# Attention scores of one token tile: two half-tile stages of four heads, or one stage of eight heads in alternation

## The chip, the cores and the metric

The kernel runs on one core of one Trainium2 chip. Five engines work side by side and meet at semaphores: TensorE (PE in the profile, its weight loads PEld), VectorE (DVE), ScalarE (ACT), GpSimd (POOL) and SyncE (SP), which here only issues DMAs. The metric is the device time of the kernel in microseconds (us); 2203.22 us is the median of three runs of the kernel before (2202.75 to 2208.09).

## The reference

Three layers follow each other, in float32, on 2304 tokens (4 batches of 576) with 512 features:

```python
k_p = k.reshape(B, H, 72, 8, D).mean(axis=3)          # keys and values pooled by 8
v_p = v.reshape(B, H, 72, 8, D).mean(axis=3)
scores = scale * np.matmul(q, k_p.transpose(0, 1, 3, 2))   # 8 heads of 64, 576 x 72
attn = softmax(scores)
x = np.matmul(attn, v_p)                               # -> 2304 x 512
x = (sigmoid(x @ w_gate) * (x @ w_val)) @ w_out        # first mixture layer, d_ff 1536
out = sum over e of P[:, e] * (relu(x @ w1[e]) @ w2[e])    # second: 8 experts, P by 8 Sinkhorn rounds
```

The change touches only the line that computes `scores`.

## The kernel before, in words

The tokens are cut into six blocks of 384 (`TB`), a block into three tiles of 128. In the first mixture layer the work is a list of 72 steps, `steps1`, one for a block j and a piece f of 128 of the 1536 inner features. A step issues, on PE, twelve matmuls for the gate ("g", L791), twelve for the value ("v"), and then the twelve of the output product of the step before it (`x2_step`, L533 to L565, shown as L543). The DVE and the ACT turn g and v into the hidden piece (L800 to L807). The second layer fills the rest of the time from about 680 us on, and is not touched.

All of it is under a schedule written out by hand: each engine executes its instructions in the order in which the program issues them. Three things are fitted into the steps.

The weights of the first layer come in as 36 wide pieces of 64-bit numbers. `narrow_tick` (L150 to L186) turns one into float32 on ACT, DVE and sometimes POOL, `split_chunk` (L213) then makes a high and a low part (L231 on ACT, `wa_lo`, L236, on DVE or POOL). The ACT queue also issues the DMA that saves the narrow form (L233), and the buffer `made` has four places, which become free only when that DMA has landed. The estimates `until["pe"]` and `until["dve"]` decide how many ticks are issued ahead of their need.

The attention of blocks 1 to 5 is the generator `attention`, cut into stages by `yield`. `slot(k, upto)` is called three times in a step: after g (k = 0), after v (k = 1) and at the step's end (k = 2). Each call adds a share, `left / (3 * (steps left) - k - 3)`, to `credit`, with `left` counted down from `STAGES`, and runs one stage for each whole credit, four at most. After the last scores of a block `hold` keeps the generator still for one or three steps. A block that is not ready when its first step begins is finished on the spot (L774).

For each tile and for g = 0 (even heads, partitions 0 to 63 of q and k) and g = 1 (odd heads, partitions 64 to 127), `scores` (L339) takes one PSUM bank, issues four head products of 64 rows, two instructions each in the trace (eight; a tile that crosses a batch has sixteen of half the width), and puts `less_max` (L367) on the list `post`: a maximum (L369) and a subtraction (L370) on DVE, which free the bank. `flush` empties the list when the next stage runs. Block 0 runs before the steps, and there `less_max` has its exponentials on ACT (L374). While the steps run, `at_bank` hands out the two banks "at" in turn; `turn_a` (transposes, L418), `values` (L433) and `after_block` (logits of a finished block, L598 to L618, through `side_bank`) use the same two. `softmax` (L389) is put on `later` after the last scores, and is issued between L804 and L807 of the next v, or at the first `turn_a` if that comes before.

Of the kernel before, what the change touches and what calls it, by code (L numbers as in the profile page):

```python
# [9 lines left out]
F32 = mybir.dt.float32  # L10
# [10 lines left out]
def attention_moe_moe_kernel(  # L21
# [31 lines left out]
    nc = tc.nc  # L53
# [7 lines left out]
    SP = S // POOL  # L61
# [23 lines left out]
    def bank(tag, bufs):  # L85
        return ps.tile([128, 512], F32, tag=tag, name=tag, bufs=bufs)
# [11 lines left out]
    def f32(ap):  # L98
        return ap.bitcast(F32)
# [38 lines left out]
    until = {"dve": 0, "pe": 0}  # L138
# [141 lines left out]
    def at_bank():  # L280

        n_bank[0] += 1
        if steps_on:
            return bank("at", 2)
        return bank(*AT_BANKS[n_bank[0] % len(AT_BANKS)])

    AT_BANKS = [("at", 2), ("big", 4), ("gv", 2), ("big", 4)]
    steps_on = []
    now = [0]
    hold = [0]  # L290

    def attention(at):
        kp, vp, qs, krs, vrs = {}, {}, {}, {}, {}
        e_ts, dens, a_ts = {}, {}, {}
# [38 lines left out]
        def pieces(j, t):  # L333

            c = j * TB + t * 128
            n = min(128, S - c % S)
            return [(0, n, c // S)] + ([(n, 128, c // S + 1)] if n < 128 else [])

        def scores(j, t, g):  # L339


            if (t, g) == (0, 0):
                e_ts[j] = at.tile([128, TPB, H, SP], F32, tag="e", name="e", bufs=1)
                dens[j] = at.tile([128, TPB, H], F32, tag="den", name="den", bufs=2)
            e_t = e_ts[j][:, t, 4 * g : 4 * g + 4]
            pt = at_bank()
            sc = pt[:, 0 : 4 * SP].rearrange("p (h s) -> p h s", h=4)
            for c0, c1, b in pieces(j, t):
                for i in range(4):
                    pr = slice(64 * g, 64 * g + 64)  # L350
                    nc.tensor.matmul(  # L351
                        out=sc[c0:c1, i],
                        lhsT=qs[j, t][pr, i, c0:c1],
                        rhs=kp[b][pr, i],
                        start=True,
                        stop=True,
                    )
            if g:
                del qs[j, t]
            elif (j, t) != (0, 0):  # L360
                load_q(j + (t + 3) // TPB, (t + 3) % TPB)
            m = at.tile([128, 4], F32, tag="mx", name="mx", bufs=4)
            until["pe"] += 900
            until["dve"] += 950
            post.append(lambda: less_max(j, t, g, sc, m, e_t))

        def less_max(j, t, g, sc, m, e_t):  # L367
            if j:
                nc.vector.tensor_reduce(out=m, in_=sc, axis=AX.X, op=ALU.max)  # L369
                nc.vector.tensor_sub(out=e_t, in0=sc, in1=m.unsqueeze(2).to_broadcast([128, 4, SP]))  # L370
                return
            nc.vector.tensor_reduce(out=m, in_=sc, axis=AX.X, op=ALU.max, negate=True)
            for i in range(4):
                nc.scalar.activation(  # L374
                    out=e_t[:, i],
                    in_=sc[:, i],
                    func=AF.Exp,
                    bias=m[:, i : i + 1],
                    accum_out=dens[j][:, t, 4 * g + i : 4 * g + i + 1],
                )  # L380


        post = []

        def flush():
            while post:
                post.pop(0)()

        def softmax(j, t):  # L389

# [75 lines left out]
        for hp in range(HP):  # L466
            load_k(1, hp)
        for t in range(TPB):
            for g in range(2):
                scores(0, t, g)  # L470
                flush()
        narrow_tick()
        narrow_tick()
        for t in range(TPB):
# [16 lines left out]
        for j in range(1, NBLK):  # L491
            b = (j * TB + TB - 1) // S
            if (j * TB - 1) // S < b:
                for hp in range(0, HP, 2):
                    pool_k(b, hp)
                    pool_k(b, hp + 1)
                    yield None
                for i in range(4):
                    pool_v(b, i)
                    if i % 2:  # L500
                        yield None
            for t in range(TPB):
                for g in range(2):
                    scores(j, t, g)
                    yield None
                    flush()
            later.append(lambda j=j: softmax(j, slice(0, TPB)))
            hold[0] = now[0] + 1 + 2 * (j > 1)
            yield None
            nb = ((j + 1) * TB + TB - 1) // S  # L510
            if j + 1 < NBLK and nb > b:
                for hp in range(HP):
                    load_k(nb, hp)
                for i in range(4):
                    load_v(nb, i)
            for t in range(TPB):
                for g in range(2):
                    turn_a(j, t, g)
                    yield None
                    flush()  # L520
                yield j
                values(j, t)
                if t < TPB - 1:
                    yield None
                flush()
            yield -1
# [183 lines left out]
    with tc.manual_schedule():  # L710
# [4 lines left out]
        at = at_pool.__enter__()  # L715
# [5 lines left out]
        def stage(upto=NBLK):  # L721

            if mark[0] is None or mark[0] < upto:
                mark[0] = next(stages, NBLK)
                n_ready[0] += mark[0] == -1
# [4 lines left out]
        def slot(k, upto):  # L730
# [9 lines left out]
            if j < NBLK:  # L740
                left = max(1, STAGES - n_stage[0])
                credit[0] = min(credit[0] + left / max(1, 3 * (at_step[j, 0] - n) - k - 3), 4)
# [2 lines left out]
                    stage(upto)  # L745
                    n_stage[0] = n_stage[0] + 1 if n_ready[0] == j else 0

        STAGES = 20

        while n_ready[0] == 0:  # L750
            stage()
# [9 lines left out]
        for n, (j, f) in enumerate(steps1):  # L761
            now[0] = n
            if (j, f) == (NBLK - 1, 0):
                assert next(stages, "end") == "end"
                at_pool.__exit__(None, None, None)
                pools["late"] = ctx.enter_context(tc.tile_pool(name="late", bufs=1, reuse_waits="tile"))
                load_w1(0)
                load_w1(1)
                first_w = prep_w1(0)
            if j == NBLK - 1 and 2 <= f < 9:  # L770
                load_xf(0, (0, 3, 4, 2, 6, 1, 5)[f - 2])
            if j == NBLK - 1 and f >= NF1 - 4:
                next(first_w, None)
            if n_ready[0] <= j:  # L774
                while n_ready[0] <= j:
                    stage()
                n_stage[0] = 0
                until["pe"] = max(until["pe"], until["dve"])
            upto = 3 if n <= at_step[0, NF1 - 1] else max(4, j + 2)
            pg = bank("gv", 2)  # L780
            pv = bank("gv", 2)
            g = base.tile([128, TB], F32, tag="g", name="g", bufs=2)
            hi, lo = h_tiles()
            for key, pt in (("g", pg), ("v", pv)):
                while (key, j, f) not in wsplit:
                    if not split_chunk() and not load_chunk():
                        narrow_tick()
                    until["pe"] = max(until["pe"], until["dve"])
                w = wsplit[key, j, f]
                mm(  # L790
                    pt[:, :TB],  # L791
                    [
                        (tuple(t[:, kk * 128 : (kk + 1) * 128] for t in w[:2]), tuple(t[:, kk] for t in xs1[j]))
                        for kk in range(KT)
                    ],
                )
                drop((key, j, f))
                until["pe"] += 2080
                if key == "g":
                    nc.scalar.activation(out=g, in_=pg[:, :TB], func=AF.Sigmoid)  # L800
                else:
                    until["dve"] = max(until["dve"], until["pe"]) + 1100
                    nc.vector.tensor_tensor(out=g, in0=g, in1=pv[:, :TB], op=ALU.mult)  # L803
                    nc.scalar.activation(out=hi, in_=g, func=AF.Copy)  # L804
                    while later:
                        later.pop(0)()
                    nc.vector.tensor_sub(out=lo, in0=g, in1=f32(hi))  # L807
                slot(key == "v", upto)
            if prev is not None:
                until["pe"] += 2080  # L810
                x2_step(*prev)
                if prev[1] == NF1 - 1:
                    gate = chain(gate, after_block(prev[0], prev[0] in (1, 3, 5)))
            gs[j, f] = (hi, lo)
            prev = (j, f)
            next(gate, None)
            slot(2, upto)
            stream(3)
# [135 lines left out]
        for n, (p, e, q) in enumerate(steps2):  # L954
# [36 lines left out]
            c1 = c_tile()  # L991
# [107 lines left out]
```

## Time and profile before

| what | value |
|---|---|
| median of three runs | 2203.22 us |
| the profiled execution | 2207.01 us, span 2205.2 us |
| PE busy | 2104.4 us (95%) |
| DVE busy | 1420.0 us (64%) |
| ACT, POOL busy | 881.9 us, 891.0 us (40% each) |
| mean granted clock of TensorE | 0.973 |

Busy shares are means over the whole span; the first layer, up to some 690 us, and the second have different limits. In a timeline row stand the start, the duration, the engine, the line of the kernel, the operation, the output and inputs by the program's names, their shape and how many instructions were merged; in brackets how long the engine sat idle before it and what it waited for.

### The profile page before, as it was taken

How to read it: one execution, taken by the hardware profiler on the slowest of the kernel's cores; microseconds unless marked ns; L12 is line 12 of the kernel's file. 1: busy time of each engine (PE TensorE's matmuls, PEld its weight loads, DVE VectorE, ACT ScalarE, POOL GpSimd, SP SyncE). 2: the span in 40 equal slices, each digit the busy share in tenths (PEclk: the TensorE clock that was granted, in tenths of full speed). 3: DMA queues.
4: the chain of work that ended last, by engine and by line, in shares of the span. 5: the costliest groups of instructions: out<-in, count | busy, mean ns of one | idle time of the engine just before them, and what ended most of it. 6: DMA issues, size and time to landing. Idle time of an engine off the chain costs nothing.

```text
span 2205.2 us, 28654 instructions
## 1 busy us (share of the span) xinstructions
PE 2104.4 (95%) x10973; PEld 1910.4 (87%) x10973; DVE 1420.0 (64%) x2162; ACT 881.9 (40%) x1607; POOL 891.0 (40%) x780
## 2 busy tenths in 40 slices
PE   4588889999999999999999999999999999999999
PEld 4478889988998898988888889888888888888888
DVE  6735787643534877666666666666666666666665
ACT  4233334344444444343434343434343434333332
POOL 1100000244454465545454545454544444454541
PEclk8679899999999999999999999999999999999999
DMA  7423453343482132212125212121224212121211
GB/s 227 150 63 110 144 167 129 125 162 130 134 290 92 58 111 81 77 58 77 58 77 186 77 58 77 59 76 59 76 65 175 93 66 74 61 77 58 77 58 39
DMA packets 87450, 222.09 MB, mean 101 GB/s; under 512 B 8848, under 2 KB 8848, under 8 KB 87312
## 3 DMA queue, kind: packets, MB, share of 16 engines
q1 hardware_dynamic: 82128, 210.81, 29.0%
q10 hardware_dynamic: 5184, 9.44, 1.1%
q8 instruction: 86, 1.41, 0.3%
q14 instruction: 52, 0.43, 0.1%
HBM read 189.55 MB, written 30.67 MB: 100 GB/s over the span
## 4 chain that ended last, share of the span: by engine, by line
PE 88%; DVE 6%; issue 2%; ACT 2%; DMA 1%; POOL 0%; SPq 0%; ACTq 0%; DVEq 0%; POOLq 0%
PE big L915 36%; PE at L884 18%; PE gv L884 14%; PE gv L268 12%; PE big L543 6%; PE at L351 1%; DVE wa_lo L236 1%; PE at L433 1%; DMA narrow<-made 1%; DVE made L166 1%; DVE wide L175 0%; PE at L268 0%; DVE g L803 0%; PE at L418 0%; ACT h L804 0%
## 5 line engine op out<-in xcount | busy, mean ns | idle before, releaser
L915 PE MATMUL big<-w2hl,h 128*128 128x512 f32 x3456 | 893.0, 394 | 0.0
L915 PEld LDWEIGHTS big<-w2hl,h 128*128 128x128 f32 x3456 | 641.2, 188 | 102.4
L944 DVE SCALAR_TENSOR_TENSOR acc<-big,prob,acc 128x512 f32<-128x512 f32 x516 | 385.5, 747 | 265.1 <-PE big L915 259.0
L688 POOL TENSOR_TENSOR fa<-raw,fa 128x768 fp32r<-128x768 f32 x96 | 179.5, 1870 | 439.5 <-PE big L915 402.7
L268 PE MATMUL gv<-xs,wa_hi 128*128 128x384 f32 x1152 | 314.7, 355 | 16.4 <-ACT xs L443 8.6
L690 POOL TENSOR_TENSOR fs<-ss,fs 128x512 fp32r<-128x512 f32 x96 | 125.1, 1303 | 292.5 <-ACT fs L687 292.5
L268 PEld LDWEIGHTS gv<-xs,wa_hi 128*128 128x128 f32 x1152 | 218.2, 199 | 23.1 <-ACT xs L443 9.5
L898 ACT ACTIVATE h<-gv 128x384 fp32r<-128x384 f32 x192 | 94.3, 491 | 357.0 <-DVE gv L1026 196.6
L884 PE MATMUL at<-xf,fa 128*128 128x384 f32 x1152 | 232.4, 336 | 0.8 <-DVE c L1019 0.8
L884 PE MATMUL at<-xf,fs 128*128 128x384 f32 x1152 | 232.4, 336 | 0.4 <-ACT c L992 0.4
L884 PE MATMUL gv<-xf,fs 128*128 128x384 f32 x1152 | 232.4, 337 | 0.0
L700 DVE TENSOR_TENSOR w2hl<-raw,w2hl 128x512 fp32r<-128x512 f32 x192 | 227.5, 1186 | 4.8 <-ACT w2hl L699 4.8
L884 PEld LDWEIGHTS at<-xf,fa 128*128 128x128 f32 x1152 | 205.6, 188 | 17.7 <-DVE c L1019 1.6
L884 PEld LDWEIGHTS gv<-xf,fs 128*128 128x128 f32 x1152 | 206.2, 189 | 16.4 <-issue 0.2
L268 PE MATMUL gv<-xs,wa_lo 128*128 128x384 f32 x576 | 202.6, 352 | 16.7 <-DVE wa_lo L236 15.1
L884 PEld LDWEIGHTS at<-xf,fs 128*128 128x128 f32 x1152 | 204.5, 188 | 9.0 <-ACT c L992 0.7
L899 DVE SCALAR_TENSOR_TENSOR h<-gv,h 128x384 fp32r<-128x384 f32 x192 | 107.1, 558 | 107.8 <-ACT h L898 107.8
L543 PE MATMUL big<-h,wa_hi 128*128 128x384 f32 x576 | 156.3, 352 | 14.4 <-DVE h L807 14.4
L577 POOL TENSOR_TENSOR fx<-x,fx 128x768 fp32r<-128x768 f32 x10 | 18.5, 1847 | 328.6 <-ACT fx L576 325.6
L268 PEld LDWEIGHTS gv<-xs,wa_lo 128*128 128x128 f32 x576 | 114.5, 199 | 20.9 <-DVE wa_lo L236 18.9
L236 POOL TENSOR_TENSOR wa_lo<-stage,wa_hi 128x512 fp32r<-128x512 f32 x67 | 98.4, 1484 | 84.1 <-ACT wa_hi L231 68.6
L691 POOL TENSOR_TENSOR fs<-ss,fs 128x512 fp32r<-128x512 f32 x96 | 125.7, 1309 | 0.0
(149 smaller groups left out, 2687.2 us busy)
## 6 DMA issues: line engine op xcount, KB each, us to landing
raw<-in_moe_w_dram SPq DMA_DIRECT2D x192, 512.0 KB, 4.4
stage<-narrow SPq DMA_DIRECT2D x150, 256.0 KB, 3.0
xd<-fx SPq DMA_DIRECT2D x21, 768.0 KB, 3.8
xf<-xd SPq DMA_DIRECT2D x21, 768.0 KB, 5.9
narrow<-made ACTq DMA_DIRECT2D x36, 256.0 KB, 3.2
wide<-in_moe_w_gate_dram SPq DMA_DIRECT2D x12, 512.0 KB, 3.7
wide<-in_moe_w_val_dram SPq DMA_DIRECT2D x12, 512.0 KB, 4.0
wide<-in_moe_w_out_dram SPq DMA_DIRECT2D x12, 512.0 KB, 11.4
```

The source lines that it names most:

```text
L236: eng.tensor_tensor(out=lo, in0=raw, in1=f32(hi), op=ALU.subtract)
L268: nc.tensor.matmul(out=out_, lhsT=a[s], rhs=b[m], start=(i == 0), stop=(i == n - 1))
L543: nc.tensor.matmul(out=x2p[d][:, :TB], lhsT=w[s][:, d * 128 : (d + 1) * 128], rhs=gs[j, f][m], start=(first and i == 0), stop=(last and i ...
L688: pl(out=fa[:, 1], in0=raw[:, 0:3], in1=f32(fa[:, 0]), op=ALU.subtract)
L690: pl(out=fs[:, 1, 0:2], in0=ss[:, 0:2], in1=f32(fs[:, 0, 0:2]), op=ALU.subtract)
L691: pl(out=fs[:, 1, 2:4], in0=ss[:, 2:4], in1=f32(fs[:, 0, 2:4]), op=ALU.subtract)
L700: nc.vector.tensor_sub(out=t[:, 1, i], in0=raw[:, i], in1=f32(t[:, 0, i]))
L884: nc.tensor.matmul(out=pt[:, :TB], lhsT=w[:, s, i, k], rhs=t[:, o, k], start=(start and m == 0), stop=(m == 5), skip_group_check=True,)
L898: nc.scalar.activation(out=t[:, 0], in_=src, func=AF.Relu)
L899: nc.vector.scalar_tensor_tensor(out=t[:, 1], in0=src, scalar=0.0, in1=f32(t[:, 0]), op0=ALU.max, op1=ALU.subtract)
L915: nc.tensor.matmul(out=py, lhsT=h[:, s, cs], rhs=w2hl[n][:, o, fh], start=(m == 0), stop=(m == 5))
L944: nc.vector.scalar_tensor_tensor(out=acc[t], in0=py, scalar=pr, in1=acc[t], op0=ALU.mult, op1=ALU.add)
```

## The change

`scores` now computes all eight heads of a tile in one stage. It takes both banks at once, and the loop over heads puts an even and an odd one in turn, each into the bank of its parity. Both `less_max` follow in one `flush`. So a block has three score stages instead of six, and `STAGES` goes from 20 to 17. `flush` and its list move out of the generator, and one more `flush` stands at the end of each step, after `x2_step` and before the step of `after_block` and the slot k = 2. The estimate for PE is 1000 a tile instead of 1800, that for DVE stays at 1900.

```diff
-        def scores(j, t, g):
+        def scores(j, t):
...
-            pt = at_bank()
-            sc = pt[:, 0 : 4 * SP].rearrange("p (h s) -> p h s", h=4)
+            scs = [at_bank()[:, 0 : 4 * SP].rearrange("p (h s) -> p h s", h=4) for g in range(2)]
             for c0, c1, b in pieces(j, t):
                 for i in range(4):
-                    pr = slice(64 * g, 64 * g + 64)
-                    nc.tensor.matmul(
-                        out=sc[c0:c1, i],
...
+                    for g in range(2):
+                        pr = slice(64 * g, 64 * g + 64)
+                        nc.tensor.matmul(
+                            out=scs[g][c0:c1, i],
...
-            until["pe"] += 900
-            until["dve"] += 950
-            post.append(lambda: less_max(j, t, g, sc, m, e_t))
+            until["pe"] += 1000
+            until["dve"] += 1900
+            for g in range(2):
+                m = at.tile([128, 4], F32, tag="mx", name="mx", bufs=4)
+                e_t = e_ts[j][:, t, 4 * g : 4 * g + 4]
+                post.append(lambda g=g, m=m, e_t=e_t: less_max(j, t, g, scs[g], m, e_t))
...
             for t in range(TPB):
-                for g in range(2):
-                    scores(j, t, g)
-                    yield None
-                    flush()
+                scores(j, t)
+                yield None
+                flush()
...
-        STAGES = 20
+        STAGES = 17
...
             gs[j, f] = (hi, lo)
             prev = (j, f)
+            flush()
             next(gate, None)
             slot(2, upto)
```

## Rows read from the trace of the kernel before

**Rows 1.** Stretches: length, busy of PE, PEld, DVE, ACT, POOL; clock, DMA share, GB/s.
```profile
70.00:120.00 50.00, 30.17 (x158) 25.91 (x156) 35.62 (x62) 15.01 (x26) 7.53 (x5) 0.73 0.47 148
120.00:200.00 80.00, 67.12 (x366) 60.39 (x367) 30.89 (x53) 29.25 (x51) 0.00 (x0) 0.79 0.32 92
200.00:300.00 100.00, 92.64 (x505) 88.54 (x504) 80.31 (x144) 34.49 (x68) 0.00 (x0) 0.93 0.41 134
```

**Rows 2.** Waits of PE from 30 to 600 us: total, times, longest.
```profile
PE at L418 <- DVE e L401: 11.3, 1, 11.3
...
PE at L351 <- DVE e L370: 4.3, 3, 1.8
```

**Rows 3.** Timeline of PE, block 4, one score stage between two products.
```profile
424.71 0.34 PE L268 MATMUL gv<-xs,wa_lo 128*128 128x384 f32 x1
424.98 1.11 PE L351 MATMUL at<-kp,qt 64*128 64x72 f32 x8
426.01 0.62 PE L268 MATMUL gv<-xs,wa_hi 128*128 128x384 f32 x2
```

**Rows 4.** Timeline of PE, block 0, both parities under way.
```profile
10.21 0.42 PE L351 MATMUL big<-kp,qt 64*128 64x72 f32 x1
10.29 0.42 PE L351 MATMUL gv<-kp,qt 64*128 64x72 f32 x1
10.43 0.42 PE L351 MATMUL big<-kp,qt 64*128 64x72 f32 x1
```

**Rows 5.** Timeline, end of a step (428 to 431 us).
```profile
428.21 0.51 PE L543 MATMUL big<-h,wa_hi 128*128 128x384 f32 x2
429.62 0.56 DVE L807 TENSOR_TENSOR h<-g,h 128x384 fp32r<-128x384 f32 x1 [0.59 <-ACT h L804]
430.10 0.45 DVE L369 TENSOR_REDUCE mx<-at 128x4 f32<-128x288 f32 x1
430.38 1.11 PE L351 MATMUL at<-kp,qt 64*128 64x72 f32 x8
```

**Rows 6.** Timeline of DVE, two less_max in a row.
```profile
71.72 0.45 DVE L369 TENSOR_REDUCE mx<-at 128x4 f32<-128x288 f32 x1
...
73.06 0.46 DVE L370 TENSOR_TENSOR e<-at,mx 128x288 f32<-128x288 f32 x1
```

**Rows 7.** Timeline, block 1: scores of its last tile, then its first transposes.
```profile
81.02 1.20 PE L351 MATMUL at<-kp,qt 64*128 64x72 f32 x8
...
86.31 0.45 DVE L369 TENSOR_REDUCE mx<-at 128x4 f32<-128x288 f32 x1
...
93.36 0.44 PE L268 MATMUL gv<-xs,wa_lo 128*128 128x384 f32 x1 [0.70 <-DVE wa_lo L236]
...
106.64 1.90 PE L418 MATMUL at<-ident,e 128*72 128x128 f32 x8 [11.26 <-DVE e L401]
```

**Rows 8.** Timeline of PE, block 2: scores at 1.2 GHz.
```profile
130.44 2.91 PE L351 MATMUL at<-kp,qt 64*128 64x72 f32 x16
...
137.41 1.98 PE L351 MATMUL at<-kp,qt 64*128 64x72 f32 x8
```

**Rows 9.** Timeline, block 3's softmax between L804 and L807.
```profile
314.31 0.55 DVE L803 TENSOR_TENSOR g<-g,gv 128x384 f32<-128x384 f32 x1
...
322.96 0.55 DVE L807 TENSOR_TENSOR h<-g,h 128x384 fp32r<-128x384 f32 x1
...
323.56 0.69 PE L543 MATMUL big<-h,wa_hi 128*128 128x384 f32 x1 [5.79 <-DVE h L807]
```

**Rows 10.** Timeline, block 5: a logits product and the scores behind it.
```profile
514.20 1.01 DVE L562 COPY x<-big 128x384 f32<-128x384 f32 x2
514.39 0.51 PE L268 MATMUL at<-fx,wg_hi 128*8 128x384 f32 x2
...
516.68 0.55 DVE L605 COPY lt<-at 8x384 f32<-8x384 f32 x1 [1.47 <-PE at L268]
...
517.28 1.11 PE L351 MATMUL at<-kp,qt 64*128 64x72 f32 x8 [0.64 <-DVE lt L605]
```

More of the change, by code (lines that the diff above doesn't have):

```diff
@@ L288, in attention_moe_moe_kernel, with flush @@
     steps_on = []
+    post = []
+    def flush():
+        while post:
+            post.pop(0)()
     now = [0]
@@ L337, in pieces @@
             return [(0, n, c // S)] + ([(n, 128, c // S + 1)] if n < 128 else [])
-        def scores(j, t, g):
-            if (t, g) == (0, 0):
+        def scores(j, t):
+            if t == 0:
                 e_ts[j] = at.tile([128, TPB, H, SP], F32, tag="e", name="e", bufs=1)
                 dens[j] = at.tile([128, TPB, H], F32, tag="den", name="den", bufs=2)
-            e_t = e_ts[j][:, t, 4 * g : 4 * g + 4]
-            pt = at_bank()
-            sc = pt[:, 0 : 4 * SP].rearrange("p (h s) -> p h s", h=4)
+            scs = [at_bank()[:, 0 : 4 * SP].rearrange("p (h s) -> p h s", h=4) for g in range(2)]
             for c0, c1, b in pieces(j, t):
                 for i in range(4):
-                    pr = slice(64 * g, 64 * g + 64)
-                    nc.tensor.matmul(
-                        out=sc[c0:c1, i],
[L353 to L360, printed above, removed]
-                load_q(j + (t + 3) // TPB, (t + 3) % TPB)
-            m = at.tile([128, 4], F32, tag="mx", name="mx", bufs=4)
-            until["pe"] += 900
-            until["dve"] += 950
-            post.append(lambda: less_max(j, t, g, sc, m, e_t))
+                    for g in range(2):
+                        pr = slice(64 * g, 64 * g + 64)
+                        nc.tensor.matmul(
+                            out=scs[g][c0:c1, i],
+                            lhsT=qs[j, t][pr, i, c0:c1],
+                            rhs=kp[b][pr, i],
+                            start=True,
+                            stop=True,
+                        )
+            del qs[j, t]
+            if (j, t) != (0, 0):
+                load_q(j + (t + 3) // TPB, (t + 3) % TPB)
+            until["pe"] += 1000
[4 more added lines that the diff above has]
+                post.append(lambda g=g, m=m, e_t=e_t: less_max(j, t, g, scs[g], m, e_t))
         def less_max(j, t, g, sc, m, e_t):
@@ L380, in less_max @@
                 )
[L383 to L387, printed above, removed]
         def softmax(j, t):
@@ L468, in attention @@
         for t in range(TPB):
-            for g in range(2):
-                scores(0, t, g)
-                flush()
+            scores(0, t)
+            flush()
         narrow_tick()
@@ L502, in attention @@
             for t in range(TPB):
-                for g in range(2):
-                    scores(j, t, g)
-                    yield None
-                    flush()
+                scores(j, t)
+                yield None
+                flush()
             later.append(lambda j=j: softmax(j, slice(0, TPB)))
@@ L815, in attention_moe_moe_kernel @@
             prev = (j, f)
+            flush()
             next(gate, None)
```

## The prediction, made before the changed kernel ran

> **What bounds the kernel now.** I read the busy times by stretch first. From 70 to 200 us TensorE is neither full nor at full speed: busy 30.2 of 50 and 67.1 of 80 us, granted clock 0.73 and 0.79, so a good part of this work runs at 1.2 GHz, the lower level; from 200 to 300 us PE (92.6%) and VectorE (80.3%) are both nearly full [rows 1]. After that PE bounds alone. The list of PE's waits came second: the scores wait only 4.3 us in all for their banks, and the longest single wait, 11.3 us, is block 1's first transpose waiting for its softmax [rows 2]. The timeline came last, for what a score stage costs and what stands behind it. So the first 300 us are a chain over several engines, in which PE time saved can turn into waiting, and from 300 to 600 us a saved PE microsecond counts.
>
> **What a visit costs, and what the pair costs.** At 2.4 GHz two products with a score stage between them start 426.01 - 424.71 = 1.30 us apart; without it they start 0.17 us apart (two merged last 0.51 us where one lasts 0.34), so a visit costs 1.13 us [rows 3, 5]. Block 0 shows what alternation does: there the stages of both parities already stand next to each other, and two instructions of the even bank start 10.43 - 10.21 = 0.22 us apart although one of the odd bank started between them at 10.29 [rows 4]. Alone, eight take 1.98 us at that clock, (1.98 - 0.42) / 7 = 0.22 us each [rows 8, 4]. The other parity is thus free: sixteen in alternation should take what eight take, 2.0 us at 1.2 GHz and 1.13 us at 2.4 GHz. The latter no row shows. Bounds: at best the second visit vanishes (-1.13 us a tile), at worst the sixteen run one behind the other and only the change of operands is saved (about -0.1 us). I take the first, the nearest row.
>
> The Trainium skill's page "TensorE: Matmul & The Clock Gate", section "Part 3: Packing small matmuls", says that matmuls start and end strictly in program order. The rows of block 0 differ: the second stage's instruction starts before the first stage has finished starting. It matters for the sum, because by the page adjacent stages would have cost 2 x 1.98 = 3.96 us, and block 2's first pair, adjacent too, took 2.91 us [rows 8]; by the page that pair would give back 1.98 us, by the trace 0.9 us; the sum would be 1.1 us lower.
>
> **What the two banks cost.** Before, a stage took one bank and the next stage the other, so DVE had a whole stage to empty a bank. Now a tile takes both, and the next tile cannot start before all four DVE operations of the one before. Two `less_max` take 73.06 + 0.46 - 71.72 = 1.80 us [rows 6]. Where they stand in DVE's queue decides. They are behind L807 of the step in which they are flushed, and the first L369 behind it starts 430.10 - 428.21 = 1.89 us after PE has begun `x2_step` [rows 5]. So both banks are free at 1.89 + 1.80 = 3.7 us after the end of v, while PE reaches slot k = 2 at 430.38 - 428.21 = 2.17 us [rows 5] and a stage at k = 1 at once.
>
> From this, each pair of successive stages: k = 0 then k = 2 of one step waits 3.7 - 2.2 = 1.5 us; k = 2 then k = 1 of the next waits 3.7 us (the flush comes only with the second stage, behind L807); two stages in one slot wait 1.8 us; with a step's end and a g product between, nothing. What is queued behind a waiting score instruction is all of PE, so its g, v and output products, and then ACT and DVE, which wait for those.
>
> **Where the stages fall.** The credit formula with `STAGES` 17 gives, by arithmetic (n is the step): block 1 n = 1 k = 1, n = 1 k = 2, n = 2 k = 0; block 2 n = 4 k = 0 and twice in k = 1; block 3 n = 15 k = 2, n = 17 k = 0, n = 18 k = 2; block 4 n = 38 k = 1, n = 39 k = 0, n = 39 k = 2; block 5 n = 48 k = 0, n = 48 k = 2, n = 49 k = 1.
>
> **Block by block.** *Block 0*: 0. The exponentials on ACT follow the even bank's last instruction, which comes no earlier.
>
> *Block 1*: the first two tiles end where they ended. The last tile, at n = 2 k = 0, is reached by PE at 81.02 us, but both banks are now needed, and the `less_max` that frees the second starts at 86.31 us, behind weight ticks [rows 7]. The new start is 86.3 + 1.8 = 88.1 us at the latest, a wait of up to 7 us, with v queued behind it. With some 2 us for the scores and 4 for v at 1.2 GHz (12 x 0.17, doubled), v ends near 94. Softmax now comes at that step's v, before the next weights, and puts L807 322.96 - 314.31 = 8.6 us behind L803, as block 3's did [rows 9]. Then come the weight ticks that stood between 86.31 and 93.36 us; of these 7 us I count 3 as ticks, an estimate, and DVE has the next weights ready near 106 instead of 93.36 us. But the transposes no longer wait 11.3 us for it: behind a g product of some 3 us they start near 109 where they started at 106.64 [rows 7]. What follows up to n = 4 is the same work in another order. Net +2.4, from -6 (the bank frees early, and the earlier softmax saves half of the 11.3) to +10 (all 7 us and a cold clock behind it).
>
> *Block 2*: its five visits take 2.91 + 4 x 1.98 = 10.8 us if all ran at 1.2 GHz and 2.91 + 4 x 1.11 = 7.4 if the four ran at 2.4 [rows 8, 3]; from the middle, 9.1, they become three of 2.0, so 3.1 saved. The waits go from 2.5 us (the 4.3 of the list without one of the longest, which is block 1's) to 3.7 + 1.8 = 5.5 [rows 2]: -0.1, bounds -4 to +4.
>
> *Block 3*: no stall, three visits of 1.13 saved in a stretch that VectorE half bounds, so about half of 3.4. Its softmax moves from n = 23 to n = 21, away from the steps that need new weights, where it held PE 5.79 us [rows 9]; there the 36 x 0.17 = 6.2 us of PE work that lie between v and the product that needs L807 cover more of its 9 us, and 3 us remain. Since the DVE work itself stays, I count 1 of the 2.8 us gained. Sum -2.7, from 0 to -6.
>
> *Block 4*: -3.4 for the visits, +1.5 for n = 39, k = 0 to k = 2: -1.9.
>
> *Block 5*: -3.4 for the visits; the wait behind the logits' copy (0.64 us) goes. At n = 48 the added flush puts `less_max` ahead of the logits, which need one of the banks: the two copies of x2 end at 515.2, so a bank is free half a 1.8 later, at 516.1, where the logits began at 514.39 [rows 10]: +1.7; the scores then wait for the logits' copy, another +0.7. The last tile, k = 2 to k = 1, waits 3.7. Sum -3.4 - 0.6 + 1.7 + 0.7 + 3.7 = +2.1. Bounds for blocks 4 and 5 together: -7.4 without any wait, +4 if the products do not overlap at 2.4 GHz.
>
> The other edits cost nothing that I can see: the earlier flush of ACT's copies stands behind x2_step, where ACT is busy 30 to 37% [rows 1]; the smaller PE estimate is about what the pair takes.
>
> **The sum.** 2.4 - 0.1 - 2.7 - 1.9 + 2.1 = -0.2 us on the profiled execution's 2207.0 (2205.2 of span and 1.8 around it), so 2206.8. That run stands 3.8 us above the median of the three, 2203.2; on the median the forecast is 2203 us.
>
> **Rivals.** A measurement here can tell about 0.3%, 6.6 us, from no change.
>
> *The waits stay small and block 1 gains.* If DVE empties the banks in time, fifteen visits go: 15 x 1.13 = 17 us, some of them at 1.2 GHz and dearer; with half of blocks 1 to 3's share lost to other waits and 4 us of the 11.3 saved, 2203 - 13 = 2190 us. For it: DVE is idle 20% and more in every stretch. Against it: the idle time is not where the flush stands, behind L807. Chance 0.27.
>
> *Block 1's last tile decides, and the case is slower.* Its 7 us wait delays v, with it ACT's L804 and the DMA issued behind it on ACT's queue, and the buffer `made` and the next weights. If the softmax's 8.6 us then come on top, and not in place of the 11.3, n = 4 starts 10 us later. Block 2's longer waits leave the clock at the lower level for one step more, which by 1.98 against 1.11 us [rows 8, 3] takes nearly twice its 6.2 us, so 5 us more. With 2 us gained elsewhere, 2203 + 10 + 5 - 2 = 2216 us. It decides from 5 us of net delay at n = 4 on. Chance 0.20.
>
> The Trainium skill's page "TensorEngine Tiling (Array Packing)", section "Performance Considerations", warns that packing speeds up TensorE and not the emptying of PSUM. That is this rival's and the forecast's mechanism: here the trace has 1.80 us of emptying against 1.13 us of products for a tile, and agrees.
>
> *The pair does not overlap at 2.4 GHz.* The nine visits after 200 us save nothing, the waits stay: the saving of 8 to 9 us counted in blocks 3 to 5 goes: 2203 + 8 = 2211 us. Block 0 speaks against it. Chance 0.05.
>
> *Forecast: savings and waits cancel.* Chance 0.48, own range 2196 to 2209 us.
>
> **How the numbers follow.** The forecast lies in the middle of the undecided band, with a part at either edge: 0.42 of its 0.48 within 0.3%, 0.04 below, 0.02 above. The faster rival gives 0.24 below and 0.03 within, the slower one 0.18 above and 0.02 within, the last 0.01 within and 0.04 above. Faster 0.28, same 0.48, slower 0.24. The range takes in most of both outer cases: 2188 to 2216 us.
>
> **What would show it.** Right: sixteen score instructions of a tile in about 1.1 us at 2.4 GHz; waits of PE's scores for L370 of some 15 us in all, where 4.3 stood, the longest before block 1's last tile; near 3.7 us at n = 49 and 1.5 at n = 39; PE's scores in total busy time near half; the 11.3 us wait shorter or gone. It is wrong if the scores wait under 6 us, or if the granted clock from 70 to 200 us moves by more than 0.05.

## The result, and the profile after

The changed kernel takes 2226.56 us (median of four runs, 2223.12 to 2227.75), the kernel before, measured beside it, 2203.97 us (2202.75 to 2208.09): ratio 1.0091, 95% interval 1.0071 to 1.0111. It is slower by some 20 us, above the range and on the side that had a chance of 0.24. The profiled execution took 2227.05 us (span 2225.3), 20.0 more than the one before, with a mean granted clock of 0.967 where 0.973 stood. The scores' own busy time on PE, from 30 to 700 us, fell from 37.08 to 24.17 us, so the products were saved. PE's busy time as a whole fell only by 6.0 us (2104.4 to 2098.4); where the other half went is not traced, other products that ran longer at the lower clock are the likely place. The rest of the loss is waiting.

In the new numbering scores is L356, less_max L375 and L376, x2_step L540, ACT's and DVE's parts of h L801 and L804, the transposes L417.

The stretches after; columns as in [rows 1], whose three stretches are the first three:
```profile
70.00:120.00 50.00, 27.70 (x146) 24.14 (x145) 32.58 (x57) 13.05 (x21) 7.51 (x5) 0.66 0.41 136
120.00:200.00 80.00, 65.75 (x383) 58.44 (x382) 34.45 (x59) 31.03 (x57) 0.00 (x0) 0.81 0.33 99
200.00:300.00 100.00, 90.72 (x516) 86.86 (x515) 79.71 (x143) 33.74 (x66) 0.00 (x0) 0.93 0.45 144
300.00:400.00 100.00, 84.63 (x474) 80.17 (x473) 65.99 (x113) 36.01 (x66) 3.68 (x2) 0.93 0.36 121
400.00:500.00 100.00, 93.36 (x599) 88.68 (x600) 57.91 (x82) 45.41 (x80) 39.16 (x25) 0.95 0.43 141
500.00:600.00 100.00, 88.15 (x543) 81.23 (x540) 41.78 (x60) 39.76 (x71) 38.16 (x26) 0.93 0.36 108
```
The last three of the same stretches before, which the prediction did not show:
```profile
300.00:400.00 100.00, 91.95 (x542) 88.17 (x541) 69.79 (x121) 40.34 (x72) 3.78 (x3) 0.97 0.42 140
400.00:500.00 100.00, 95.81 (x614) 90.51 (x613) 55.94 (x80) 45.76 (x82) 43.86 (x28) 0.98 0.44 142
500.00:600.00 100.00, 95.99 (x600) 88.65 (x598) 45.84 (x67) 45.86 (x82) 44.91 (x30) 1.00 0.42 135
```
Up to 300 us, where the prediction looked for the danger, PE is busy only 1.4 to 2.5 us less in each stretch. The loss stands where PE had been nearly full: 7.3 us of PE less in 300 to 400, 7.8 in 500 to 600, both at a lower clock.

What PE waits for after, from 30 to 700 us (total, times, longest):
```profile
PE gv L268 <- DVE wa_lo L236: 26.1, 8, 6.4
PE big L540 <- DVE h L804: 18.2, 4, 5.2
PE at L356 <- issue: 13.7, 4, 6.3
PE gv L268 <- ACT wa_hi L231: 12.2, 6, 3.2
...
PE at L356 <- DVE e L376: 2.5, 6, 0.6
...
PE at L268 <- DVE e L376: 1.7, 1, 1.7
...
PE at L356 <- PE at L356: 0.7, 1, 0.7
PE at L356 <- PE big L540: 0.7, 1, 0.7
```
and the same view before:
```profile
PE gv L268 <- DVE wa_lo L236: 15.1, 9, 4.3
PE big L543 <- DVE h L807: 14.4, 4, 5.8
...
PE gv L268 <- ACT wa_hi L231: 6.4, 6, 2.2
...
PE at L351 <- issue: 2.0, 1, 2.0
```
Three things grew: waits for weights (L236 and L231: 21.5 to 38.3 us), the waits for h, and the scores' wait for their banks. That last is put down to "issue", or to an instruction of PE, where a stage's first instruction waits; in the timeline each of these starts 0.1 us after an L376 of DVE has ended, so it is a bank's wait: 13.7 + 2.5 + 0.7 + 0.7 = 17.7 us for the scores and 1.7 for block 5's logits. Before, the "issue" of 2.0 us is such a wait too (it ends 0.1 us after an L370), so 2.0 + 4.3 [rows 2] = 6.3 us stood there, and not the 4.3 that the prediction read. The 11.3 us before block 1's transposes [rows 2] are gone.

To place the loss I take, in each trace, the time at which a step's `x2_step` begins, and subtract that of the kernel before. Each row rests on one profiled execution, so that 1 or 2 us in it say nothing.

```
x2_step of step   7     21    34     46     50     60
after            -1.1  -2.9   +8.6   +9.6  +14.3  +20.1
e_order          -1.2  -0.8  +11.1  +13.0  +18.0  +23.5
e_now            -6.5  -8.5   -0.2   -2.4   -6.4   -1.4
e_pe1800         +0.9  -4.1   -4.6   -5.5   -0.8   +4.8
e_later          -2.6  -4.7   -2.2   +6.9  +13.9  +13.9
f_before_pe      +1.6  +6.3  +14.5  +15.7  +15.7  +15.7
e_now_pe        -10.9 -11.6  -13.1  -15.3  -19.2  -14.0
g_now_pe_swap   -10.4 -10.0  -14.5  -17.2  -21.1  -20.9
g_before_swap    +1.0  +1.2   +0.3   +2.1   +2.0   +0.2
h_order          -9.1  -9.2  -11.6  -11.1  -14.0   -8.8
h_before_now     -7.1  -2.8   -4.1   -4.2   -5.2   -5.2
```

Blocks 1 and 2 lie before step 7, block 3's scores and softmax between 7 and 21, block 4's before 42, block 5's scores at steps 48 and 49 and its softmax at 50. Of the +20.1, -1.1 come up to step 7, -1.8 up to 21, **+11.5 from 21 to 34**, +1.0 up to 46, **+4.7 from 46 to 50** and **+5.8 from 50 to 60**. After that the difference stays (+20.0 at step 71).

### The profile page after: what moved, and what is told of

The parts are those of the page before. It is cut to its first block, busy times and chain, and to the rows that moved or that the text cites. A ratio compares the mean times of both kernels' runs of the same rounds, so it can differ in the third digit from the quotient of the medians.

```text
span 2225.3 us, 28648 instructions
## 1 busy us (share of the span) xinstructions
PE 2098.4 (94%) x10973; PEld 1904.8 (86%) x10973; DVE 1425.0 (64%) x2162; ACT 881.9 (40%) x1607; POOL 891.5 (40%) x780
## 4 chain that ended last, share of the span: by engine, by line
PE 86%; DVE 7%; issue 3%; ACT 2%; DMA 1%; POOL 0%; SPq 0%; ACTq 0%; DVEq 0%; POOLq 0%
PE big L913 36%; PE at L882 18%; PE gv L882 13%; PE gv L268 11%; PE big L540 5%; PE at L432 1%; DVE wa_lo L236 1%; DVE made L166 1%; DVE g L800 1%; PE at L356 1%; DVE wide L175 1%; DMA narrow<-made 1%; ACT h L801 0%; PE at L268 0%; DMA wide<-in_moe_w_gate_dram 0%
## 5 line engine op out<-in xcount | busy, mean ns | idle before, releaser
L687 POOL TENSOR_TENSOR fs<-ss,fs 128x512 fp32r<-128x512 f32 x96 | 125.0, 1302 | 292.5 <-ACT fs L684 292.5
L882 PEld LDWEIGHTS at<-xf,fa 128*128 128x128 f32 x1152 | 205.6, 188 | 17.7 <-DVE c L1017 1.6
L540 PE MATMUL big<-h,wa_hi 128*128 128x384 f32 x576 | 157.6, 355 | 18.2 <-DVE h L804 18.2
L236 POOL TENSOR_TENSOR wa_lo<-stage,wa_hi 128x512 fp32r<-128x512 f32 x67 | 98.9, 1491 | 89.7 <-ACT wa_hi L231 68.9
L540 PEld LDWEIGHTS big<-h,wa_hi 128*128 128x128 f32 x576 | 110.7, 201 | 20.5 <-DVE h L804 19.5
## 6 DMA issues: line engine op xcount, KB each, us to landing
wide<-in_moe_w_out_dram SPq DMA_DIRECT2D x12, 512.0 KB, 10.5
```

The source lines that it names most:

```text
L236: eng.tensor_tensor(out=lo, in0=raw, in1=f32(hi), op=ALU.subtract)
L540: nc.tensor.matmul(out=x2p[d][:, :TB], lhsT=w[s][:, d * 128 : (d + 1) * 128], rhs=gs[j, f][m], start=(first and i == 0), stop=(last and i ...
L687: pl(out=fs[:, 1, 0:2], in0=ss[:, 0:2], in1=f32(fs[:, 0, 0:2]), op=ALU.subtract)
L882: nc.tensor.matmul(out=pt[:, :TB], lhsT=w[:, s, i, k], rhs=t[:, o, k], start=(start and m == 0), stop=(m == 5), skip_group_check=True,)
```

## The experiments

Those on the changed kernel first. The ratio is that to the kernel before on the same chip; kernels measured on different chips are compared by their ratios.

**e_order: the eight heads one parity behind the other, all else as after.**
```
             for c0, c1, b in pieces(j, t):
-                for i in range(4):
-                    for g in range(2):
+                for g in range(2):
+                    for i in range(4):
```


> The changed kernel with the two loops over heads swapped: first the four even heads of a tile, then the four odd ones, still one stage and both banks. If the alternation is what saves PE time, sixteen instructions at 2.4 GHz take about 1.75 us instead of 1.11 (adjacent parities overlap in part, as block 0 showed before) and the kernel is 4 to 8 us slower than the changed one, 2231 to 2235 us. If alternation is worth nothing here (the pair is bound by something both orders share, or the saving is lost behind waits anyway), it stays within 2 us of 2226.6.

Measured: 2231.91 us (2229.34 to 2232.35), ratio 1.0103 (1.0071 to 1.0135). The two timelines of PE, block 4, e_order and then after:
```profile
438.19 1.62 PE L356 MATMUL at<-kp,qt 64*128 64x72 f32 x16
...
444.13 1.63 PE L356 MATMUL at<-kp,qt 64*64 64x72 f32 x32
```
```profile
435.64 1.11 PE L356 MATMUL at<-kp,qt 64*128 64x72 f32 x16
436.69 0.62 PE L540 MATMUL big<-h,wa_hi 128*128 128x384 f32 x2
...
441.06 1.03 PE L356 MATMUL at<-kp,qt 64*64 64x72 f32 x32
```
In alternation sixteen take what eight took [rows 3], 1.11 us; one parity behind the other they take 1.62. Busy time of the scores from 30 to 700 us is 24.17 us after, 32.62 here, 37.08 before. So the alternation works on PE and is not what made the kernel slower. What it is worth in time this run doesn't show: the medians differ by 5.4 us, as was expected, but the ratios by 0.12% (under 3 us), and their intervals overlap. h_order, below, shows it.

**e_now: each tile's `less_max` issued in its own stage, ahead of L804 and softmax.**
```
                 scores(j, t)
-                yield None
                 flush()
+                yield None
```


> The changed kernel with less_max issued in the stage itself, right behind the scores, before the yield, so that it stands in front of the next weight ticks and of L807 in VectorE's queue. Theory A (the waits of a tile's scores for both banks make the loss): the scores' waits fall from 16 us to under 4, block 5's 3.3 us wait at n = 49 and the slow x2_step behind it go, and the kernel comes to 2214 to 2218 us. Theory B (the loss is the softmax that moved to earlier steps, where it holds weights and output products): the waits go all the same, but the time stays over 2222 us.

Measured: 2207.35 us (2201.77 to 2209.78), ratio 1.0000 (0.9983 to 1.0016): more than was expected. The scores' waits became
```profile
PE at L356 <- issue: 3.2, 2, 1.6
...
PE at L356 <- DVE e L376: 1.1, 2, 0.6
```
and in block 5 the banks are free long before the next stage:
```profile
506.63 1.11 PE L356 MATMUL at<-kp,qt 64*128 64x72 f32 x16
...
507.77 0.46 DVE L375 TENSOR_REDUCE mx<-at 128x4 f32<-128x288 f32 x1 [1.59 <-PE at L356]
...
509.12 0.46 DVE L376 TENSOR_TENSOR e<-at,mx 128x288 f32<-128x288 f32 x1
...
511.28 0.56 DVE L804 TENSOR_TENSOR h<-g,h 128x384 fp32r<-128x384 f32 x1 [0.59 <-ACT h L801]
...
511.95 0.52 PE L268 MATMUL at<-fx,wg_hi 128*8 128x384 f32 x2
...
520.24 1.12 PE L356 MATMUL at<-kp,qt 64*128 64x72 f32 x16
...
521.92 0.51 PE L540 MATMUL big<-h,wa_hi 128*128 128x384 f32 x2
```
Its bank waits are 3.2 + 1.1 = 4.3 us where after has 19.3 with the logits'. From step 46 to 50 it gains 4.0 us where after loses 4.7. So DVE was not too slow for the two banks: the emptying was issued too late. What is left of the loss, +8.3 from step 21 to 34 and +5.0 from 50 to 60, has other causes.

**e_pe1800: the estimate for PE back at 1800 a tile.**
```
-            until["pe"] += 1000
+            until["pe"] += 1800
```


> The changed kernel with the planner's estimate for PE set back to 1800 a tile, which alone decides how many weight ticks are issued ahead. By step 24 it issues a few ticks more than the changed kernel. If block 3's late weights (9.7 us of waits after 325 us) come from that estimate, they go and the kernel comes to 2216 to 2220 us. If they come from the softmax's new place, it stays within 3 us of 2226.6.

Measured: 2211.52 us (2207.12 to 2213.61), ratio 1.0013 (0.9999 to 1.0026), again more than was expected. PE's waits from 322 to 372 us, first after, then e_pe1800:
```profile
PE gv L268 <- DVE wa_lo L236: 6.8, 3, 2.9
PE gv L268 <- ACT wa_hi L231: 2.9, 2, 1.7
```
```profile
PE gv L268 <- DVE wa_lo L236: 1.6, 2, 1.2
...
```
The 1.6 are what the kernel before waits there. The loss from step 21 to 34 goes from +11.5 to -0.5. Counted in the programs, by the end of step 21 the kernel before has issued 92 weight ticks (calls of `narrow_tick`), after 90, e_pe1800 100.

**f_before_pe: the kernel before with the smaller estimate alone, 500 a stage.**
```
-            until["pe"] += 900
+            until["pe"] += 500
```


> The kernel before with one edit, the planner's estimate for PE at 500 a score stage instead of 900 (1000 a tile, as the change has it). If the estimate alone makes block 3's weights late, this kernel loses 5 to 11 us, 2209 to 2217 us, with waits for wa_lo and wa_hi after 325 us. If it hurts only together with the softmax's earlier place (step 21 instead of 23), it stays within 3 us of the kernel before.

Measured: 2220.32 us (2213.24 to 2222.95), ratio 1.0051 (1.0035 to 1.0066). That is 11 us by the ratio and 13 by the medians, at the upper end of the first case or above it. No score is moved or merged, and half of the loss comes at the same place: +8.2 us from step 21 to 34, with 83 ticks issued by the end of step 21. Another +6.3 come before step 21, and what makes them was not followed. In 322 to 372 us most of the same waits stand:
```profile
PE gv L268 <- DVE wa_lo L236: 4.4, 2, 2.9
PE gv L268 <- ACT wa_hi L231: 2.0, 2, 1.2
```
So the estimate, for which the prediction charged nothing, is a part of the change with a price of its own.

**e_now_pe: both repairs.**

> Both repairs together: less_max issued in the scores' own stage, and the PE estimate back at 1800 a tile. Theory: the loss of the change is two separate things, block 3's late weights (11.5 us between steps 21 and 34, from the estimate) and the bank waits with what follows them in block 5 (10.5 us, from the place of the flush); if so, what stays is the saving of the products, and the kernel comes to 2194 to 2199 us, clear of the kernel before. Rival: both repairs act on the same waits in the first 300 us and don't add; then 2203 to 2208 us, no better than the first repair alone.

Measured: 2192.40 us (2191.18 to 2195.34), ratio 0.9930 (0.9916 to 0.9945). That is more than was expected. By the ratios, e_now gains 0.91%, e_pe1800 0.78% and both together 1.61%: they nearly add up, and the change now gains. The scores' busy time is 20.36 us, 0.55 of before. What remains is +5.2 us between step 50 and 60.

**e_later: the softmax of blocks 3 to 5 two stages later, all else as after.**
```
+            if j > 2:
+                yield None
+                yield None
             later.append(lambda j=j: softmax(j, slice(0, TPB)))
```


> The changed kernel with two empty stages ahead of the softmax's entry in blocks 3 to 5, so that the softmax is issued at steps 24, 42 and 52 (before the change 23, 42 and 52; in the changed kernel 21, 41 and 50). Theory B: block 5's wait of the output product for L807 (5.2 us) goes back to about 1.8 and block 3's waits for weights after 325 us (9.7 us) go under 4, so 2212 to 2218 us. Theory A: the bank waits stay and the kernel stays over 2221 us.

Measured: 2224.31 us (2221.23 to 2227.77), ratio 1.0073 (1.0044 to 1.0101): missed. The softmaxes of blocks 3, 4 and 5 came at steps 24, 42 and 52 (after 21, 41 and 50; before 23, 42 and 52). Block 5's then cost nothing (0.0 from step 50 to 60, +5.8 after), but the two stages more also moved block 4's scores, which lost 9.1 us between steps 34 and 46. One edit moved two things, so of this run only the reading from step 50 to 60 and the waits of block 3 are used.

**g_now_pe_swap and g_before_swap: the softmax behind L804 instead of ahead of it, in e_now_pe and in the kernel before (there L807).**
```
+                    nc.vector.tensor_sub(out=lo, in0=g, in1=f32(hi))
                     while later:
                         later.pop(0)()
-                    nc.vector.tensor_sub(out=lo, in0=g, in1=f32(hi))
```


> Both repairs, and the softmax issued behind the subtraction that makes the low part of h (L804 in the changed kernel) instead of ahead of it. Theory: each softmax holds that subtraction for about 9 us and the output product waits for it (5.2 us at the longest, 17 us in all with block 2's); with the subtraction first these waits go, and the kernel comes 6 to 14 us under the one with both repairs. Rival: the wait only moves to the weights behind the softmax in VectorE's queue; then within 3 us of it.

> The kernel before with the softmax issued behind L807 instead of ahead of it, nothing else. Its waits of the output product for L807 are 14.4 us in all. If they are on the path, it gains 6 to 12 us (2192 to 2198 us), and this gain has nothing to do with the change; if the weights behind take their place, within 3 us of the kernel before.

Measured: 2187.25 us (2186.49 to 2187.85), ratio 0.9904 (0.9887 to 0.9920), and 2206.05 us (2201.99 to 2209.44), ratio 0.9986 (0.9975 to 0.9998). In the first, step 50 to 60 goes from +5.2 to +0.2, as it should if the softmax ahead of L804 is the cause; the total gains 5 us, between the two cases (6 to 14, and within 3). In the kernel before the same edit moves the wait and hardly the time, as its rival had it. There the waits for L807 (14.4 us) go, those for weights stood at 15.1 and those of L433 at 3.7 us, and now:
```profile
PE gv L268 <- DVE wa_lo L236: 20.1, 9, 4.7
...
PE at L433 <- ACT a L420: 10.6, 7, 5.1
```
g_now_pe_swap is the best version found, 0.96% under the kernel before.

**h_order: e_now_pe with the loops as in e_order.**

> The kernel with both repairs (2192.4 us), with the loops over heads swapped: first the even heads, then the odd ones. In the changed kernel this swap cost 5 us. If the alternation's saving is real and no longer lost, it costs at least as much here, 2197 to 2202 us; the rest of the distance to the kernel before is then the single visit instead of two. If the order of the heads is hidden once the waits are gone, it stays at 2191 to 2195 us.

Measured: 2197.10 us (2195.90 to 2198.06), ratio 0.9958 (0.9943 to 0.9972), against 0.9930 in alternation: 5 us by the medians, 6 by the ratios, as was expected. Here the alternation's worth is shown; the same 5 us that the expectation names for the changed kernel are there only in the medians.

**h_before_now: the kernel before with `less_max` in its own stage.**
```
                     scores(j, t, g)
-                    yield None
                     flush()
+                    yield None
```


> The kernel before with less_max issued in its own score stage, ahead of the yield. Before, the scores waited 4.3 us for their banks in all, so if the place of the flush matters only because a tile takes both banks, this stays within 4 us of the kernel before; if an early less_max is a gain of its own, it comes 6 us or more under it.

Measured: 2201.73 us (2198.79 to 2210.35), ratio 0.9979 (0.9964 to 0.9995). That is 5.8 us by the medians and about 4.6 by the ratio, between the two cases and undecided. The same edit gained some 20 us after the change, so about a quarter of that was to be had before, and by the table in blocks 1 and 2 (-7.1 at step 7).

## Why the prediction was wrong, step by step

*What held.* The pair overlaps at 2.4 GHz: 1.11 us, forecast 1.13. The rule for the banks held in every block. Forecast and measured: up to 7 and 6.5 us for block 1's last tile, 3.7 and 1.8 against 3.2 and 1.0 in block 2, 1.5 against 1.2 at n = 39, 1.7 against 1.67 for the logits, 3.7 against 3.3 at n = 49. With 2.6 us before block 1's second tile, which was there before (2.0), that is 19.3 us in all. Block 5's last tile:
```profile
525.87 0.51 PE L268 MATMUL at<-fx,wg_hi 128*8 128x384 f32 x2 [1.67 <-DVE e L376]
...
537.00 0.41 PE L356 MATMUL at<-kp,qt 64*128 64x72 f32 x2 [2.77 <-issue]
537.90 1.68 PE L356 MATMUL at<-kp,qt 64*128 64x72 f32 x14 [0.49 <-DVE e L376]
539.52 1.01 PE L540 MATMUL big<-h,wa_hi 128*128 128x384 f32 x2
```
It waits 2.77 + 0.49 = 3.3 us, where 3.7 were forecast. DVE in that stretch shows why, L375 stands behind L804 and the first bank is free with the first L376's end:
```profile
535.48 0.56 DVE L804 TENSOR_TENSOR h<-g,h 128x384 fp32r<-128x384 f32 x1 [0.59 <-ACT h L801]
535.96 0.45 DVE L375 TENSOR_REDUCE mx<-at 128x4 f32<-128x288 f32 x1
536.44 0.46 DVE L376 TENSOR_TENSOR e<-at,mx 128x288 f32<-128x288 f32 x1
...
537.30 0.46 DVE L376 TENSOR_TENSOR e<-at,mx 128x288 f32<-128x288 f32 x1
```
Block 1 went as told: its last tile waits, the next weights come at 104.06 us (near 106), so that PE now waits 6.18 us for them where 0.70 stood [rows 7], and the transposes start at 107.43 us (109) without the long wait for softmax:
```profile
85.75 0.67 PE L356 MATMUL at<-kp,qt 64*128 64x72 f32 x2 [6.27 <-issue]
...
104.06 0.69 PE L268 MATMUL gv<-xs,wa_lo 128*128 128x384 f32 x1 [6.18 <-DVE wa_lo L236]
...
107.43 1.38 PE L417 MATMUL at<-ident,e 128*72 128x128 f32 x8
```
Blocks 1 and 2 together came to -1.1 us (forecast +2.3). The slower rival's mechanism is therefore not what made the kernel slower, though its wait is there. The scores' busy time fell to 0.65 of before, not near half (0.55 in e_now_pe). The faster rival's sum doesn't come out as written: 17 less 5 and plus 4 is 16, not 13, hence 2187 us and not 2190. The clock test was mixed: -0.07 from 70 to 120 us, +0.02 from 120 to 200.

*What failed first: "the smaller PE estimate is about what the pair takes" and so costs nothing.* As an estimate of PE's time it was right (1.11 us for a tile), and as a part of the change it had one of the two large prices: set back, it gains 17 us by the ratios, and in the kernel before it costs 11. `until["pe"]` decides how many weight ticks run ahead, and the 1800 a tile had bought a lead that covers what the estimates don't see. Without it block 3's weights come late: from step 7 to 34 the forecast for block 3 was -2.7, and -1.8 + 11.5 = +9.7 came. The softmax alone washes out, where 1 us of gain was counted: at step 22, when after and e_pe1800 have paid for theirs (PE waits 4.95 and 4.5 us) and the kernel before has not, they stand at +5.7 and +3.9; at step 24, when all have, e_pe1800 is back at -4.6, where it was at step 21 (-4.1). After stands at +3.3 there and goes on to +8.6 by step 28, and that is the weights: e_pe1800 removes it, f_before_pe makes it alone. The programs' order of issue says which weights: when step 25 begins, `split_chunk` has issued 59 pieces in the kernel before and in e_pe1800, and 58 in after, e_now and f_before_pe; at step 29 it is 65 against 64. PE waits there: after, 1.7 + 2.4 us ahead of step 25's products and 2.9 + 1.2 ahead of step 29's, and e_pe1800 0 and 0.4 + 1.2. e_later, which has 59 and 64, waits nothing at step 25 and the same 2.9 + 1.2 us at step 29. A further wait of 1.5 us at step 28, in these kernels and not in e_pe1800, has no such difference behind it. Part of the loss is the clock, 0.93 from 300 to 400 us instead of 0.97 before and in e_pe1800, which the runs don't separate from the waits.

*What failed second: block 5, forecast +2.1, measured +10.5.* Two terms were left out. Behind the 3.3 us wait x2_step runs at the lower clock: two merged last 1.01 us above, 0.51 in [rows 5], and it takes 4.1 us from 539.52; in e_now, where the wait is gone, the same x2_step takes 2.3 us (two merged 0.51, at 521.92 above). And the softmax moves from step 52 to 50. The forecast followed block 3's softmax to its new step and not block 5's. At step 52 a logits product stood between v and x2_step; at step 50 nothing does, and PE waits out the rest of the softmax:
```profile
560.52 0.69 PE L540 MATMUL big<-h,wa_hi 128*128 128x384 f32 x1 [5.17 <-DVE h L804]
```
on DVE,
```profile
556.17 3.83 DVE L400 TENSOR_TENSOR e<-e,den 128x576 f32<-128x576 f32 x3
...
559.92 0.55 DVE L804 TENSOR_TENSOR h<-g,h 128x384 fp32r<-128x384 f32 x1
```
and before, where the wait was short and the three products faster:
```profile
PE big L543 <- DVE h L807: 1.8, 1, 1.8
```
```profile
554.85 2.10 DVE L401 TENSOR_TENSOR e<-e,den 128x576 f32<-128x576 f32 x3
556.87 0.55 DVE L807 TENSOR_TENSOR h<-g,h 128x384 fp32r<-128x384 f32 x1
```
The traces also show why L400 takes 3.83 us where 2.10 stood: at step 50 its first two operations run beside POOL's subtractions for the weights,
```profile
555.72 2.99 POOL L236 TENSOR_TENSOR wa_lo<-stage,wa_hi 128x512 fp32r<-128x512 f32 x2
```
In all twelve traces the 28 operations of this form that ran beside an L236 of POOL took 1.43 to 1.84 us each, the 152 others 0.74 to 0.76. They are those of blocks 4 and 5 in the seven kernels that issue these softmaxes at steps 41 and 50. So of the 3.3 us by which the wait grew (1.8 to 5.17), 1.7 are this meeting, which came with the new step; no run moved it by itself. e_later (softmax back at step 52) and g_now_pe_swap (softmax behind L804) both take this term to about nothing.

*Block 4, forecast -1.9, measured +1.0.* Its bank wait was right (1.2 us for 1.5). Its softmax moved from step 42 to 41 and met POOL in the same way, and the wait for it grew from 3.9 to 5.2 us. So the forecast had the bank waits right, and missed what the smaller estimate, the clock behind a wait and the softmaxes of blocks 4 and 5 at their new steps would cost.

*What stays open.* e_now gained some 20 us, where the waits for banks that it removes (19.3 to 4.3 us) explain some 15; the rest may be the clock behind them, but no run separates it. h_before_now lies between its two cases. The split by steps rests on one execution each, while the totals rest on timed runs.

## What to carry to other kernels

An estimate in a schedule written out by hand is not only a guess at a duration: it steers how much is issued ahead, and a more exact one can take away a lead that nothing else gives, so change it alone and time it. When two stages become one that takes both buffers, move the emptying into the same stage, ahead of whatever else the emptying engine has queued. When stages vanish, follow every later piece of work that moves up with them, and ask what covered it where it stood.

## What the runs showed of the hardware

Two parities of 64-row products, issued in alternation, overlap at 2.4 GHz: sixteen take 1.11 us, as eight do alone, and 32 of half the width 1.03; one parity behind the other they take 1.62 and 1.63. The Trainium skill's rule that matmuls start strictly in program order ("TensorE: Matmul & The Clock Gate", "Part 3: Packing small matmuls") would let none of the second parity start before all of the first have started. The trace agrees that the order in which they are issued counts (1.62 against 1.11 us), and not that it is strict: in [rows 4] an instruction of the odd bank starts at 10.29 us, ahead of one of the even bank at 10.43 that was issued before it.

A wait of 3.3 us on PE was followed by an x2_step of 4.1 us at the lower clock, where 2.3 us stand without the wait, so that it cost some 2 us beyond itself. By stretches it is not so plain: in four of the six above PE's busy time and the granted clock both fall with the change, but from 120 to 200 us PE is busy less at a higher clock (0.79 to 0.81), and from 200 to 300 us at the same (0.93).

A product of 128x576 numbers on DVE took 0.75 us with POOL idle and 1.43 to 1.84 us beside a subtraction on POOL.
